# Nyström attention and a squared-ReLU feed-forward on one core: batch 0's A computed with whole-tile exponentials, another rule for warm-up products, and a new order table

## The chip, the cores and the metric

The kernel runs on 1 core of one Trainium2 chip. The metric is device time in microseconds (us) from launch to end, the median of several runs. A profiled execution has a time of its own and a span, which goes from its first to its last instruction. The five engines run instruction queues of their own: TensorE (PE; its weight loads are PEld), VectorE (DVE), ScalarE (ACT), GpSimd (POOL) and SyncE (SP). Each works its queue strictly in order and waits on semaphores for the others.

## The reference

For 8 batches of 8 heads (576 tokens, head size 64, 32 landmarks) the attention is approximated through landmark means, and its output goes through a two-layer feed-forward with the square of a ReLU between the layers.

```python
q_lm = q.reshape(B, H, m, S // m, D).mean(axis=3)      # m = 32, 18 tokens each
k_lm = k.reshape(B, H, m, S // m, D).mean(axis=3)
A = sm(q, k_lm); Bm = sm(q_lm, k_lm); C = sm(q_lm, k)  # sm: scaled softmax over the last axis
Z = Bm.T / (norm_1(Bm) * norm_inf(Bm) + 1e-06)
for _ in range(6):
    Z = 2 * Z - Z @ Bm @ Z
x = (A @ Z @ C @ v)                                    # then 4608 tokens x 512
h = x @ w_in                                           # 512 x 2048
out = (np.maximum(h, 0.0) ** 2) @ w_out                # 2048 x 512
```

## The kernel before, in words

The kernel is one core's program over the 8 batches. Nothing is scheduled by the compiler. Every piece of work is an "op" with a name, declared with `op(...)`, and the long string `ORDER` (line 1239) lists all names. `name@n` gives the PSUM banks, and `/A`, `/D`, `/P` put an op on ACT, DVE or POOL in place of its usual engine. `Plan.schedule` (line 100) walks the list once with rough durations and gives each op a planned start, and the program is emitted in that order with real semaphores between engines. So an engine's queue is the list, read for that engine alone.

The names that matter here, with the batch b as first number:

- Loads, all issued by POOL on one software queue: `ldq`, `ldk` (queries and keys, tile X, line 426), `ldv` (V, line 442), `win` (a quarter of w_in in two halves, line 450; `win10` and `win11` are quarter 1), `wout` (a quarter of w_out, line 457), `lx` (another view of q and k for the landmark sums of batches 3 to 7, XS, line 432).
- Attention: `T` (32x32 block transposes of q and k, DVE, line 471), `lm`/`lme`/`lmt` (landmark means on PE, eviction, transpose), `B…` (the softmax of Bm and its norms, many short DVE steps), `BBT`, `Yi`, `Zi` and then six rounds `N` on PE (line 718 for batches 0 and 1, 713 later) and `U` on DVE (line 727) for Z; in batches 2 to 7 each `N` also needs `bd` (line 650). `SC`/`SS` are the scores of C (and of A from batch 2 on), `Cmx`, `Cex`, `CT` their softmax, `CV` = C times V, `Zd`, `Zm`, `ZC` the product with Z, `W` = (Z C V) times w_in by quarters, evicted by `We` into the tile WP.
- A in batches 0 and 1, in two parts u = 0 (256 tokens of each half) and u = 1 (320): `bk` builds a block-diagonal operand (line 961), `SA` the scores on PE, then `Amx` (row maximum, line 974), `Asb` (subtract, line 985), `Aex` (exponential, ACT, line 987), `Asu`, `Arc` (sum and reciprocal), `Aml` (scale, line 994), `Ap` (transpose on PE, line 1005), `Ab` (eviction to the tile AT). Batch 0 cuts each of them in two, a and b.
- Feed-forward: `F` (AT times WP, line 1079; four products of 256 or 320 columns for batch 0, f + 16 being part u = 1), `R` (ReLU eviction, ACT or DVE), `Q` (square into the tile G), `O` (G times w_out, line 1126, four products of 512 columns each), `Oe` and `St` (eviction and store).

In batch 0 before, the part u = 1 takes another way through the exponential: `BY_ROW` (line 1229) names it, and `rows` (line 978) issues ten ACT exponentials of 32 columns for each half, each with its row's negated maximum (tile NM) as bias, so that no `Asb` is needed there. The row maxima of a and of b go to two tiles, NM1a and NM1b.

While TensorE has nothing to do early on, `Plan.fillers` (line 161) puts products of constants into the gaps of the planned PE times (line 1200, tile onesb), up to the first `O0` op. It takes an op's end as its start plus its duration.

Of the kernel before, what the change touches and what calls it, by code (L numbers as in the profile page):

```python
# [54 lines left out]
class Plan:  # L55
# [105 lines left out]
    def fillers(self, until, width, emit):  # L161
# [3 lines left out]
        for o in ops:  # L165
            a, b = o.start, o.start + o.engs["PE"]
# [43 lines left out]
def a_(n):  # L210
    return 0.1 + 0.00084 * n
# [53 lines left out]
def kernel(  # L265
# [32 lines left out]
    XS = mk("XS", [96, 2, H, 6, D], BF16)  # L298
# [22 lines left out]
    NM = {k: mk("NM" + "".join(map(str, k[1:])), [P, 10], F32) for k in BY_ROW}  # L321
# [139 lines left out]
    def attention(b):  # L461
# [17 lines left out]
        def landmarks_rows():  # L479
# [3 lines left out]
            def lmx(e):  # L483
                xs = XS[:].rearrange("p t (r c) j d -> p t r c j d", r=2)
# [7 lines left out]
               lambda e: copy(e, lm[:], view(), scale=LMS), R=[pl_], W=[("LM", i2, r) for r in range(2)])  # L492

# [445 lines left out]
        for u in range(2) if b in TOKENS else ():  # L939
# [27 lines left out]
            cuts = [0, 2 * n, 4 * n] if b in FIRST else [0, 4 * n]  # L967
            for j, (x0, x1) in enumerate(zip(cuts, cuts[1:])):
# [3 lines left out]
                by_row = (b, u, z) in BY_ROW  # L972
                op(f"Amx{b}.{u}{z}", {"DVE": v_(w)}, lambda e, s3=s3, p3_=p3_, pS=pS, at=at, neg=NM.get((b, u, z)):
                   nc.vector.tensor_reduce(s3(0)[:, at] if neg is None else neg[:, 0:at.stop - at.start],
                                           p3_(pS)[:, at], axis=AX.X, op=ALU.max, negate=neg is not None),
                   R=[pS], W=kx_("amx"))

                def rows(e, nm=NM.get((b, u, z)), sa3=sa3, p3_=p3_, pS=pS, x0=x0, x1=x1):
                    for x in range(x0, x1):
                        nc.scalar.activation(sa3[:, x], p3_(pS)[:, x], AF.Exp, bias=nm[:, x - x0:x - x0 + 1])  # L980
# [181 lines left out]
    def loads(what, b):  # L1162
# [53 lines left out]
ROWS = (3, 4, 5, 6, 7)  # L1216
SQ_POOL = (0,)
# [11 lines left out]
BY_ROW = ((0, 1, "a"), (0, 1, "b"))  # L1229
# [10 lines left out]
c0 ldk0.1 c1 ldq0.1 ldq0.0 ldk0.0 ldq1.0 ldk1.0 c2 ldk1.1 c12 c3/A c11 c5 T0.11 ldq1.1 ldv0.00  # L1240
ldv0.10 T0.01 c9/A lm0.1@1 c6/A c17 lmc0.10 lmc0.11/D ldv0.11 lme0.1 lmt0.1 T0.00 SC0.1@2 win00
T0.10 lm0.0@0 Cmx0.1 Bce0@6 win01 lme0.0 Cex0.1 lmt0.0 T1.00 bk0/P B0@4 SC0.0@0 c15/A Bmx0 Bsb0
CT0.1 Bex0 win11 Bsu0 SA0.1@2 Brc0 Cmx0.0 Bml0/P Bmb0/A c13 win10 Bcs0 Btr0 Cex0.0 Amx0.1a BBT0@5
Bnm0 SA0.0@7 Brn0 Aex0.1a c8 Yi0 Zi0/P Amx0.1b win21 Amx0.0b N0.0@0 lm1.0@4 U0.0 Amx0.0a Asb0.0b
N0.1@1 Aex0.1b lm1.0a U0.1 win20 Asb0.0a CT0.0 N0.2@6 lm1.0b U0.2 T1.01 win31 N0.3@5 lme1.0 win30
U0.3 CV0@6,0 Aex0.0a Asu0.1a lmt1.0 Asu0.0a bk1/P CVe0.0/A B1@2 Asu0.1b N0.4@4 c10 Aex0.0b U0.4
Bmx1 Arc0.1a Bsb1 N0.5@5 Asu0.0b Aml0.1a/P Bex1 SA1.1@6 c14/A Bsu1 Arc0.1b Brc1 CVe0.1/A Crc0
U0.5 wout0 Cmk0 Aml0.1b CR0@2 Amx1.1 Zd0@4 Bml1/P CRe0/A Bmb1/A Zm0 Ap0.1@2 Blo1 Arc0.0a Arc0.0b
Asb1.1 Aml0.0a/P Bcs1@0 Ab0.1/A SA1.0@5 Btr1 Aml0.0b/P Aex1.1 Bnm1 Bad1 BBT1@3 Brn1 ldv1.11 ZC0@4
Yi1 Ap0.0@7 Zi1 ZCe0 Amx1.0 wout1 N1.0@6 Ab0.0/A W0.1@2 U1.0 W0.0@0 ldk2.1 Asb1.0 We0.1 N1.1@4  # L1250
wout2 W0.2@6 U1.1 We0.01/D We0.00 ldk2.0 N1.2@5 F0.4@2 We0.2 U1.2 ldq2.0 F0.2@0 R0.4/D F0.0@4
# [120 lines left out]
```

## Time and profile before

| what | value |
|---|---|
| time, median of 3 runs | 259.07 us (259.05 to 259.97) |
| profiled execution, its own time | 259.55 us |
| its span | 257.8 us |
| PE, DVE, ACT, POOL busy | 248.5, 211.5, 176.3, 71.5 us |
| granted TensorE clock, mean | 0.999 |
| DMA moved | 34.18 MB, mean 133 GB/s |
| first F product starts | 30.49 us |
| first O product starts | 34.80 us |
| products of constants | 43 |

A row of the timeline reads: start in us, length in us, engine, line of the kernel, operation, tile written and tiles read, shape, count of merged instructions, and in brackets how long the engine stood idle before and what ended that. Rows of a stretch ("30.50:34.80 4.30, …") give its length and then the busy time and count of PE, PEld, DVE, ACT and POOL in that order, the granted clock, the share of the DMA engines and GB/s.

### The profile page before, as it was taken

To read this page: it belongs to the slowest core of one execution; us is meant where nothing else is said; L and a number is where in the kernel's file an instruction comes from. 1 tells how busy PE (TensorE), PEld (TensorE's weight loads), DVE (VectorE), ACT (ScalarE), POOL (GpSimd) and SP (SyncE) were. 2 spreads that over 40 slices of the span, in tenths; PEclk is the share of its full clock that TensorE was granted. 3 is DMA by queue.
4 is the path that set the end of the run, shared out by engine and by line. 5 is a ranking of instruction groups with operands and counts; after the bars stand their busy time and mean duration, and the time that the engine had idled before them with its cause. 6 is when DMAs were issued, how large, how long until landed. Compare 5 with 4: busy or idle time off the path is not lost.

```text
span 257.8 us, 7581 instructions
## 1 busy us (share of the span) xinstructions
PE 248.5 (96%) x3093; PEld 140.5 (54%) x3093; DVE 211.5 (82%) x549; ACT 176.3 (68%) x343; POOL 71.5 (28%) x122
## 2 busy tenths in 40 slices
PE   6979999999999999999999999999999999999993
PEld 2546565557554567465555466465454575466542
DVE  2779897987999999998998999888999989667221
ACT  3465779669896898888566499596663897357300
POOL 8566846643353260550210400021100100000000
PEclk9999999999999999999999999999999999999999
DMA  6999999999999999899613991025100350231044
GB/s 100 200 191 201 204 210 208 208 224 233 235 203 220 221 212 220 137 202 223 154 21 69 170 205 30 4 45 122 43 3 3 81 123 3 57 79 31 4 106 97
DMA packets 25123, 34.18 MB, mean 133 GB/s; under 512 B 2432, under 2 KB 14464, under 8 KB 25088
## 3 DMA queue, kind: packets, MB, share of 16 engines
q0 software_dynamic: 19168, 24.25, 55.6%
q1 hardware_dynamic: 5760, 9.31, 14.2%
q8 instruction: 24, 0.39, 0.6%
q10 hardware_dynamic: 160, 0.13, 0.2%
q14 instruction: 11, 0.09, 0.1%
HBM read 48.50 MB, written 9.44 MB: 225 GB/s over the span
## 4 chain that ended last, share of the span: by engine, by line
PE 84%; DVE 7%; DMA 3%; POOL 2%; issue 1%; ACT 1%; POOLq 0%
PE ps L1126 46%; PE ps L1079 23%; PE ps L906 3%; DMA X<-in_q_dram 3%; PE ps L835 2%; PE ps L487 1%; PE ps L749 1%; DVE SA L1032 1%; PE ps L713 1%; POOL X L426 1%; PE ps L1005 1%; PE ps L1200 1%; ACT SA L980 1%; PE ps L744 1%; PE ps L718 1%
## 5 line engine op out<-in xcount | busy, mean ns | idle before, releaser
L1126 PE MATMUL ps<-w_out,G 128*128 128x512 bf16 (+1 forms) x592 | 138.3, 374 | 0.0
L1126 PEld LDWEIGHTS <-G 128*128 128x128 bf16 x592 | 54.0, 98 | 54.7 <-issue 5.8
L1100 ACT ACTIVATE RS<-ps 128x576 bf16<-128x576 f32 (+2 forms) x104 | 63.7, 652 | 13.3 <-PE ps L1079 8.9
L1079 PE MATMUL ps<-AT,WP 128*128 128x288 bf16 (+2 forms) x512 | 72.0, 286 | 0.0
L1079 PEld LDWEIGHTS <-WP 128*128 128x128 bf16 x512 | 48.6, 98 | 20.6 <-issue 1.9
L1107 ACT ACTIVATE G<-RS 128x576 bf16<-128x576 bf16 (+2 forms) x54 | 35.9, 686 | 2.0 <-DVE RS L1102 1.6
L1109 DVE TENSOR_TENSOR G<-RS 128x576 bf16<-128x576 bf16 (+2 forms) x72 | 31.1, 447 | 6.8 <-ACT RS L1100 6.4
L471 DVE STREAM_TRANSPOSE TT<-X 128x576 uint32<-128x576 uint32 x32 | 24.0, 759 | 4.8 <-DMA X<-in_k_dram 4.2
L413 ACT CAST WP<-ps 128x1024 bf16<-128x1024 f32 (+1 forms) x23 | 21.8, 978 | 7.9 <-PE ps L906 7.8
L413 ACT COPY OS<-ps 128x512 f32<-128x512 f32 (+1 forms) x25 | 14.2, 571 | 18.1 <-PE ps L1126 18.0
L650 POOL TENSOR_TENSOR BD<-ST,blkb 128x256 bf16<-128x256 bf16 x15 | 10.9, 725 | 46.5 <-DVE ST L727 46.5
L790 ACT ACTIVATE C<-ps,sm 128x576 bf16<-128x576 f32 x16 | 14.4, 904 | 12.3 <-DVE sm L787 11.9
L1102 DVE TENSOR_SCALAR RS<-ps 128x576 bf16<-128x576 f32 (+2 forms) x24 | 17.9, 747 | 5.5 <-PE ps L1079 4.7
L442 POOL DMA_DIRECT2D V<-in_v_dram x24 | 12.9, 539 | 18.4 <-PE ps L835 15.1
L417 DVE COPY OS<-ps 128x512 f32<-128x512 f32 x12 | 8.3, 689 | 9.8 <-PE ps L1126 9.8
L727 DVE SCALAR_TENSOR_TENSOR ST<-ST,ps 128x128 bf16<-128x128 bf16 (+1 forms) x48 | 12.7, 264 | 2.6 <-PE ps L713 2.4
L1200 PE MATMUL ps<-onesb 128*128 128x512 bf16 (+1 forms) x38 | 11.9, 402 | 1.5 <-DVE onesb L349 1.5
L787 DVE TENSOR_REDUCE sm<-ps 128x1 f32<-128x576 f32 x16 | 11.8, 741 | 1.4 <-PE ps L718 1.2
L417 DVE CAST WP<-ps 128x1024 bf16<-128x1024 f32 (+1 forms) x11 | 12.2, 1119 | 0.3 <-PE ps L906 0.2
L1032 DVE STREAM_TRANSPOSE SA<-ps 128x320 f32<-128x320 f32 (+1 forms) x24 | 10.1, 456 | 0.3 <-PE ps L744 0.3
L906 PE MATMUL ps<-w_in,ZC 64*32 64x512 bf16 x256 | 10.2, 382 | 0.0
L426 POOL DMA_DIRECT2D X<-in_q_dram x16 | 8.9, 559 | 4.5 <-DVE sm L644 2.5
(144 smaller groups left out, 292.2 us busy)
## 6 DMA issues: line engine op xcount, KB each, us to landing
out_dram<-OS SPq DMA_DIRECT2D x70, 128.0 KB, 2.5
X<-in_k_dram POOLq DMA_DIRECT2D x16, 288.0 KB, 8.9
X<-in_q_dram POOLq DMA_DIRECT2D x16, 288.0 KB, 10.3
XS<-in_k_dram POOLq DMA_DIRECT2D x5, 576.0 KB, 9.6
XS<-in_q_dram POOLq DMA_DIRECT2D x5, 576.0 KB, 7.5
V<-in_v_dram POOLq DMA_DIRECT2D x8, 288.0 KB, 8.8
w_in<-in_moe_w_in_dram POOLq DMA_DIRECT2D x8, 256.0 KB, 10.3
w_out<-in_moe_w_out_dram POOLq DMA_DIRECT2D x4, 512.0 KB, 10.1
```

Source lines behind the costliest of these rows:

```text
L413: nc.scalar.copy(o, i)
L417: eng(e).tensor_copy(o, i)
L471: op(f"T{b}.{t}{r}", {"DVE": v_(576) + 0.02}, lambda e, r=r: nc.vector.transpose(tt[:, t, r].rearrange("p s m e -> p (s m e)").bitcast(U32 ...
L790: op(f"Cex{b}.{r}", {"ACT": a_(576) + 0.27}, lambda e, r=r: nc.scalar.activation(Cs[r][:].rearrange("p x u -> p u x"), cbanks(r), AF.Exp, ...
L906: nc.tensor.matmul(ps[quad(pos_a(c, r)), pW.at + r, :], lhsT=zcs[r][half, pos_c(c, r), :], rhs=w_in[half, c, 512 * ch:512 * ch + 512], sta ...
L1079: nc.tensor.matmul(ps[:, ph.at + i, 0:w], lhsT=wp[:, r, 128 * ff:128 * ff + 128], rhs=at[:, r, t0:t0 + w], start=(r == 0), stop=(r == 1))
L1100: nc.scalar.activation(rs, pair(ph, w), AF.Relu)
L1102: nc.vector.tensor_scalar(out=rs, in0=pair(ph, w), scalar1=0.0, scalar2=None, op0=ALU.max)
L1107: nc.scalar.activation(g, rs, AF.Square)
L1109: eng(e).tensor_tensor(g, rs, rs, ALU.mult)
L1126: nc.tensor.matmul(bank(po)[:, 0:c1 - c0], lhsT=G[:, f, lo:lo + P], rhs=w_out[:, f, c0:c1], start=(f == 0), stop=(f == NF - 1))
L1200: nc.tensor.matmul(ps[:, j, 0:w], lhsT=onesb[:, 0:P], rhs=x[:, 0:w], start=True, stop=True)
```

## The change

Four things are edited. The last covers the whole table.

First, `BY_ROW` is empty, so batch 0's part u = 1 goes through `Amx`, `Asb`, one `Aex` of 320 columns for each half, as u = 0 does: 20 ACT instructions become 2, and DVE gains the two subtractions `Asb0.1a` and `Asb0.1b`. Second, in `fillers` a PE op now ends where the plan says, with the wait for the next block of instructions that the plan counts for it, and not at start plus duration; 38 products of constants remain of 43. Third, the code for landmark sums added up by the DMA (`load_sums`, `landmarks_added`, `ADDED`) comes in, but `ADDED` is empty, so that it issues nothing; XS gets 128 partitions in place of 96, of which 96 are used. Fourth, `ORDER` is written anew for all batches.

```diff
-            a, b = o.start, o.start + o.engs["PE"]
+            a, b = o.start, o.end
...
-    XS = mk("XS", [96, 2, H, 6, D], BF16)
+    XS = mk("XS", [P, 2, H, 6, D], BF16)
...
-    NM = {k: mk("NM" + "".join(map(str, k[1:])), [P, 10], F32) for k in BY_ROW}
+    NM = mk("NM", [P, 20], F32)
...
+            by_row = (b, u) in BY_ROW
+            if by_row:
+                op(f"Amx{b}.{u}", {"DVE": v_(128 * n)}, lambda e, nm=NM, p3_=p3_, pS=pS, n=n: nc.vector.tensor_reduce(
+                    nm[:, 0:4 * n], p3_(pS), axis=AX.X, op=ALU.max, negate=True),
+                   R=[pS], W=[("NM", z) for z in range(2)])
...
                 if by_row:
-                    op(f"Aex{b}.{u}{z}", {"ACT": ROW * (x1 - x0)}, rows, R=[pS, *kx_("amx")], W=kx_("sa"))
+                    op(f"Aex{b}.{u}{z}", {"ACT": ROW * (x1 - x0)}, rows, R=[pS, ("NM", j)], W=kx_("sa"))
                 else:
+                    op(f"Amx{b}.{u}{z}", {"DVE": v_(w)}, lambda e, s3=s3, p3_=p3_, pS=pS, at=at:
+                       nc.vector.tensor_reduce(s3(0)[:, at], p3_(pS)[:, at], axis=AX.X, op=ALU.max),
+                       R=[pS], W=kx_("amx"))
                     op(f"Asb{b}.{u}{z}", {"DVE": v_(w)}, lambda e, sa3=sa3, p3_=p3_, pS=pS, b3=b3, at=at:
...
+ADDED = ()
+ADD_COST = 1.5
...
-BY_ROW = ((0, 1, "a"), (0, 1, "b"))
+BY_ROW = ()
...
-U0.5 wout0 Cmk0 Aml0.1b CR0@2 Amx1.1 Zd0@4 Bml1/P CRe0/A Bmb1/A Zm0 Ap0.1@2 Blo1 Arc0.0a Arc0.0b
+CVe0.0/A Aml0.0a/P T1.01 N0.4@5 CRe0/A CVe0.1/A wout0 U0.4 Asb0.1a bk1 B1@6 Aex0.1a ldq2.1
```

On PE the new table reads, from the end of batch 0's Z on: `N0.5 B1 Ap0.0 Zd0 SA1.0 ZC0 SA1.1 W0.1 W0.3 Ap0.1 F0.6 W0.0 F0.4 Bcs1 F0.20 F0.2 F0.0 F0.18 W0.2 F0.22 F0.16 F0.12 F0.14 O1.0 BBT1 F0.28 …`. The old one read `N0.5 SA1.1 CR0 Zd0 Ap0.1 Bcs1 SA1.0 BBT1 ZC0 Ap0.0 N1.0 W0.1 W0.0 N1.1 W0.2 N1.2 F0.4 F0.2 F0.0 W0.3 F0.18 F0.6 F0.22 F0.20 F0.10 O1.0 F0.24 …`. So part u = 0 of A comes first where u = 1 did, and batch 1's `BBT1`, `N1.0`, `N1.1` and `N1.2` have gone from ahead of the F products to behind the first O products. The pieces that follow show three other queues.

The first place is ACT's queue between the joint C V and the first ReLU evictions (L980 and L987 before, L1013 after are the exponentials, AT the eviction of A, ZC that of Z C V, WP that of W, RS the first ReLU). Before:

```order
L413 CAST Bb_107<-Bf_105 128x64
L413 CAST AT_80<-ps 128x640
L987 ACTIVATE SA_76<-SA_76 128x640
L413 CAST ZC_0_90<-ps 128x128
L413 CAST AT_80<-ps 128x512
L413 CAST WP_94<-ps 128x2x512
L413 CAST WP_94<-ps 128x512
```

And after:

```order
L1013 ACTIVATE SA_76<-SA_76 128x320 x2
L415 CAST AT_80<-ps 128x512
L607 ACTIVATE Bl_103<-Bl_103 128x64
L415 CAST ZC_0_90<-ps 128x128
L415 CAST Bb_107<-Bf_105 128x64
L1013 ACTIVATE SA_77<-SA_77 128x512
L415 CAST WP_94<-ps 128x2x512 x2
L1126 ACTIVATE RS_128<-ps 128x512
```

Between the eviction of Z C V and the first eviction of W now stand batch 1's `Bmb1` (Bb) and the exponential `Aex1.0` (SA_77, 512 columns); before, it was the eviction `Ab0.0` (AT, 512) alone. The two exponentials of batch 0's u = 1 (the first row, 320 columns) now stand behind C V, where before their twenty stood ahead of it. The eight copies of cpick, which stood second in ACT's queue before, now stand between the two exponentials of u = 0.

The second place is POOL's queue from the last quarter of w_in to the second half of w_out (An is `Aml`'s output, BK `bk`'s, w_out and X are loads). Before:

```order
L450 DMA w_in_123<-in_moe_w_in_dram 64x4x512 x4
L961 TENSOR_TENSOR BK_143<-LT1_75,blkw_142 128x512
L994 TENSOR_TENSOR An0_78<-SA0_76,smA0_119 128x320
L457 DMA w_out_124<-in_moe_w_out_dram 128x4x512
L590 TENSOR_TENSOR Bf1_105<-Bl1_103,sm1_118 128x64
L994 TENSOR_TENSOR An1_79<-SA1_77,smA1_120 128x256 x2
L442 DMA V1_66<-in_v_dram 32x1152
L457 DMA w_out_124<-in_moe_w_out_dram 128x4x512
```

And after:

```order
L462 DMA w_in_122<-in_moe_w_in_dram 64x4x512 x4
L1020 TENSOR_TENSOR An1_79<-SA1_77,smA1_120 128x256 x2
L469 DMA w_out_123<-in_moe_w_out_dram 128x4x512
L428 DMA X2_64<-in_q_dram 128x1152
L454 DMA V1_66<-in_v_dram 32x1152
L1020 TENSOR_TENSOR An0_78<-SA0_76,smA0_119 128x320
L469 DMA w_out_123<-in_moe_w_out_dram 128x4x512
L648 TENSOR_TENSOR Blo_108<-Bf1_105,Bb1_107 128x64
L1020 TENSOR_TENSOR An0_78<-SA0_76,smA0_119 128x320
```

The scalings of u = 0 (An1) moved ahead of those of u = 1 (An0), `bk1` (BK) went to DVE, and the last scaling, on which `Ap0.1` waits, now stands behind the issue of `wout1` (the second w_out row) and `Blo1`. Before it was on DVE.

The third place is DVE's queue while batch 2's Z is worked out and batch 1's F products begin (L727 and L750 are `U`; TT0 and TT1 are the transposes `T` of batches 2 and 3; BD is `bd`). Before:

```order
L671 TENSOR_TENSOR ST0_0_96<-Bf0_104,sm0_117 128x2x32
L471 STREAM_TRANSPOSE TT1_69<-X0_62 128x576
L727 SCALAR_TENSOR_TENSOR ST0_1_97<-ST0_0_96,ps_61 128x128
L417 CAST WP1_95<-ps_61 128x512
L417 CAST WP1_95<-ps_61 128x2x512
L471 STREAM_TRANSPOSE TT1_69<-X0_62 128x576
L727 SCALAR_TENSOR_TENSOR ST0_0_96<-ST0_1_97,ps_61 128x128
```

And after:

```order
L673 TENSOR_TENSOR BD0_100<-ST0_0_96,blkb_145 128x256
L483 STREAM_TRANSPOSE TT0_68<-X2_64 128x576
L1128 TENSOR_SCALAR RS1_126<-ps_61 128x512
L750 SCALAR_TENSOR_TENSOR ST0_1_97<-ST0_0_96,ps_61 128x128
L483 STREAM_TRANSPOSE TT1_69<-X0_62 128x576 x2
L750 SCALAR_TENSOR_TENSOR ST0_0_96<-ST0_1_97,ps_61 128x128
L673 TENSOR_TENSOR BD0_100<-ST0_0_96,blkb_145 128x256
```

One transpose of batch 2 came into this stretch, and a third one of batch 3 stands a little further on, 12 rows behind the last one printed and still ahead of the scores `SS2.0`, where before two of batch 3's four stood here and two behind the scores.

236 lines of the change are left out of this document (129 added, 107 removed).

## The prediction, made before the changed kernel ran

> **What bounds the kernel now.** First the page: the busy line (engine, us, share of the span, instructions) and the chain of work that ended last.
>
> ```profile
> PE 248.5 (96%) x3093; PEld 140.5 (54%) x3093; DVE 211.5 (82%) x549; ACT 176.3 (68%) x343; POOL 71.5 (28%) x122
> PE 84%; DVE 7%; DMA 3%; POOL 2%; issue 1%; ACT 1%; POOLq 0%
> ```
>
> TensorE is busy for 248.5 of 257.8 us and is 84% of the chain. A share is an average, so next I read the stretches of the span (start:end, length, then busy us and count of PE, PEld, DVE, ACT, POOL, granted clock, DMA share, GB/s).
>
> ```profile
> 15.00:20.00 5.00, 3.81 (x60) 2.44 (x59) 3.61 (x14) 4.42 (x22) 2.59 (x6) 1.00 1.08 180
> 30.50:34.80 4.30, 4.30 (x41) 3.07 (x41) 3.81 (x9) 4.14 (x7) 2.33 (x5) 1.00 1.21 205
> 34.80:64.30 29.50, 29.50 (x414) 17.72 (x411) 24.14 (x64) 21.80 (x43) 15.44 (x25) 1.00 1.17 217
> 64.30:80.30 16.00, 15.39 (x206) 8.00 (x206) 15.53 (x44) 14.84 (x28) 8.59 (x14) 1.00 1.18 217
> 120.80:253.90 133.10, 132.97 (x1483) 73.50 (x1481) 107.33 (x255) 84.25 (x151) 10.88 (x18) 1.00 0.35 70
> ```
>
> From the first F product on, PE is full in these rows but in 64.3 to 80.3, where 0.61 us is missing. So the time is the moment at which this stream starts, plus fixed PE work, plus what stalls it. The clock is 1.00 even at 15 to 20 us, where PE is emptiest. PE's timeline gives the start of the stream, the price of its pieces, and its two stalls (start, length, engine, line, operation; in brackets idle before and releaser).
>
> ```profile
> 28.17 0.66 PE L1005 MATMUL ps<-ident,An 128*128 128x128 bf16 x4
> 30.49 1.53 PE L1079 MATMUL ps<-AT,WP 128*128 128x256 bf16 x12
> 31.95 0.41 PE L906 MATMUL ps<-w_in,ZC 64*32 64x512 bf16 x8
> 34.80 1.03 PE L1126 MATMUL ps<-w_out,G 128*128 128x512 bf16 x4
> 35.66 1.69 PE L1079 MATMUL ps<-AT,WP 128*128 128x320 bf16 x12
> 40.33 1.03 PE L1126 MATMUL ps<-w_out,G 128*128 128x512 bf16 x4
> 41.29 0.70 PE L749 MATMUL ps<-TT,LT 32*32 32x288 bf16 x32
> 41.81 0.24 PE L718 MATMUL ps<-ST 32*32 32x64 bf16 x8
> 41.98 2.76 PE L1126 MATMUL ps<-w_out,G 128*128 128x512 bf16 x12
> 64.65 0.28 PE L749 MATMUL ps<-TT,LT 32*32 32x288 bf16 x1
> 65.50 0.27 PE L744 MATMUL ps<-TT,LT 32*32 32x256 bf16 x1 [0.56 <-ACT RS L1100]
> 79.56 0.30 PE L749 MATMUL ps<-TT,LT 32*32 32x288 bf16 x1
> 79.91 0.27 PE L744 MATMUL ps<-TT,LT 32*32 32x256 bf16 x1
> ```
>
> An O quarter takes 0.86 in the stream (34.80 to 35.66). An F of u = 1 takes 0.54: twelve products run 1.69 including the last one's drain of about 0.15. An F of u = 0 takes by the same reading (1.53 − 0.15) / 3 = 0.46; I use 0.44, since the drain of a last product is nearer 0.2. At 40.33 + 0.86 = 41.19 the quarter is through and the 32x32 scores start at 41.29: a change of tile shape costs 0.10. An N (L718) with its change back takes 0.17 (41.81 to 41.98). The two stalls are 65.50 − 64.65 and 79.91 − 79.56, less such a change and the first product's 0.1: about 0.64 and 0.14, together 0.78.
>
> **The head: what frees it.** The row exponentials hold ACT, and DVE waits for them.
>
> ```profile
> 5.33 2.01 ACT L413 COPY cpick<-identf 32x64 f32<-32x64 f32 x8
> 15.67 1.87 ACT L980 ACTIVATE SA<-ps,NM1a 128x32 f32<-128x32 f32 x10
> 18.10 1.89 ACT L980 ACTIVATE SA<-ps,NM1b 128x32 f32<-128x32 f32 x10 [0.56 <-DVE NM1b L974]
> 22.30 0.42 ACT L987 ACTIVATE SA<-SA 128x256 f32<-128x256 f32 x1
> 26.99 0.74 ACT L987 ACTIVATE SA<-SA 128x640 f32<-128x640 f32 x1 [0.25 <-DVE SA L985]
> 17.57 0.49 DVE L974 TENSOR_REDUCE NM1b<-ps 128x10 f32<-128x320 f32 x1 [1.33 <-ACT SA L980]
> 18.31 0.28 DVE L727 SCALAR_TENSOR_TENSOR ST<-ST,ps 128x128 bf16<-128x128 bf16 x1
> 24.02 0.20 DVE L727 SCALAR_TENSOR_TENSOR ST<-ST,ps 128x64 bf16<-128x64 bf16 x1
> 19.36 0.42 DVE L985 TENSOR_TENSOR SA<-ps,smA 128x256 f32<-128x256 f32 x1
> 26.13 0.77 DVE L985 TENSOR_TENSOR SA<-ps,smA 128x640 f32<-128x640 f32 x1
> ```
>
> Removed: 1.87 + 1.89 = 3.76 of ACT. Added: two exponentials of 320 columns, between 0.42 (256) and 0.74 (640), so 0.48 each, and on DVE two subtractions between 0.42 and 0.77, 0.49 each. But the 2.01 of cpick copies, which ran when ACT was free, now stands between u = 0's exponentials, so ACT's net relief here is 3.76 − 0.96 − 2.01 = 0.8. More matters on DVE: its idle 1.33 ahead of NM1b goes, and with it `U0.0` moves from 18.31 to about 16.9, and `U0.5`, the last step of Z, from 24.02 to about 22.5 (the chain N, U between them is unchanged, and DVE gains in it about what it loses). `bk1` is on DVE now, which no row shows; its bounds are 0.28 (`bd`, half as wide) and POOL's 1.17 for the same work. I take 0.42, nearer the DVE row.
>
> ```profile
> 25.49 0.41 DVE L861 TENSOR_TENSOR ZM<-ps,CRS 128x256 bf16<-128x256 f32 x1
> 29.26 0.68 DVE L985 TENSOR_TENSOR SA<-ps,smA 128x512 f32<-128x512 f32 x1
> 29.41 2.42 ACT L413 CAST WP<-ps 128x1024 bf16<-128x1024 f32 x3
> 23.31 0.73 POOL L994 TENSOR_TENSOR An<-SA,smA 128x320 bf16<-128x320 f32 x1
> 33.58 0.75 POOL L457 DMA_DIRECT2D w_out<-in_moe_w_out_dram  x1 [1.95 <-DMA w_out<-in_moe_w_out_dram]
> DMA to landing us min/median/max: 9.9/10.3/11.5
> L650 DVE TENSOR_TENSOR BD<-ST,blkb 128x256 bf16<-128x256 bf16 x21 | 5.9, 282 | 0.4
> 12.57 1.17 POOL L961 TENSOR_TENSOR BK<-LT,blkw 128x512 bf16<-128x512 bf16 x1
> ```
>
> Following that through: `Zm0` is at about 23.2 (was 25.49). `Asb1.0` moves up between `Zm0` and batch 1's norms and ends at 26.0 instead of 29.94. On ACT, `Aex1.0` and then `We0.1` follow at about 26.7 to 27.6 (was 29.41 to 30.4). Thus W is no longer what the first F waits for.
>
> **What is late next.** `F0.6` also needs `Ab0.1`, and so the transposes `Ap0.1`, and they need POOL's last scaling `Aml0.1b`, which stands behind three DMA issues: a load of X and one of V (shorter than a load of w_out, and taken while nothing waits) and `wout1`. The last one reuses the semaphore of the load eight before it, the last quarter of w_in, issued at about 15 in the new order; at 9.9 to 11.5 to landing (the row for those loads) it is free between 25.0 and 26.5. The row at 33.58, where a w_out issue held POOL for 1.95, shows that such a wait happens. Then `wout1` 0.75, `Blo1` (64 columns) 0.3 at most beside An's 0.73 for 320, and `Aml0.1b` 0.73: POOL is through between 26.8 and 28.3. With 0.66 for `Ap0.1` and what is left of the eviction, `F0.6` can start between 27.7 and 29.0. I take 28.6. Behind the waiting issue nothing else on POOL is urgent; DVE and ACT don't wait for it except through that eviction.
>
> From `F0.6` to `O1.0` the new order has six F of u = 0 (2.64), four of u = 1 (2.16), `W0.0` and `W0.2` (0.34 each, 31.95 to 32.29, with its change of shape) and `Bcs1` (0.28 at most, as it is no longer than those): 5.8. So `O1.0` starts at 34.4 to 34.5, with the bounds 33.75 (27.7 + 5.8, and 0.25 since W's evictions, 2.42 for three, then pace the first F) and 34.9; I take 34.45, against 34.80. What stands ahead of `O1.0` differs: F0.12, F0.14 and F0.16 came in and F0.10 went out (+0.98), `BBT1` and three N went behind it (−0.91: 0.17 for each, an estimated 0.06 more for the change ahead of it and what a thin piece loses at both ends). **Head: 34.80 − 34.45 + 0.07 = −0.42.**
>
> **Changes of tile shape.** In the stream behind `O1.0` I count 97 for 86, where batch pieces are now split by single O quarters; seven of the eleven are the moved `BBT1` and N, priced above, so four are new: 4 × 0.10 = **+0.38**. The Trainium skill, "TensorEngine Tiling (Array Packing)", section "Key Properties", says that changing the tiling mode, not just the tile, drains TensorE, and so speaks against finer interleaving. The row at 41.29 agrees, with 0.10; the sum would be the same by either.
>
> **The old stalls.** The 0.56 wait at 65.50 was for the ReLU that held the second bank of `SS2.1`. In the new order `O5.2`, `N2.5` and `O5.3` (0.86 + 0.1 + 0.86) stand between `SS2.0` and `SS2.1`, longer than the whole wait, and at 79.91 a similar step. **−0.78**, or nothing if the bank is late by as much again.
>
> **DVE ahead of `SS2.0`.** The batch-2 landmarks and transposes are the second place where it can go wrong.
>
> ```profile
> 54.70:64.30 9.60, 9.60 (x134) 5.97 (x130) 7.58 (x22) 8.65 (x17) 3.55 (x6) 1.00 1.15 236
> L471 DVE STREAM_TRANSPOSE TT<-X 128x576 uint32<-128x576 uint32 x32 | 24.0, 759 | 4.8 <-DMA X<-in_k_dram 4.2
> ```
>
> DVE is idle for 9.60 − 7.58 = 2.02 there, and the new order brings a net two transposes, 2 × 0.76 = 1.52, into it: 0.5 is left. They wait for X, too; its loads were issued earlier than before, which helps. I put +0.35 on all new stalls of the stream (none is shown by the trace; bounds 0 and the 1.52 of the transposes). The rest of the stream, the constants' 38 for 43 products and the wider XS, costs nothing on PE: the former lie in gaps of the head, and XS's new partitions hold nothing.
>
> **Sum.** −0.42 + 0.38 − 0.78 + 0.35 = −0.47 against the profiled run's own 259.55 (span 257.8 and 1.75 around it): 259.1. That run lies 0.48 over the median of 259.07, so on the median **258.6**.
>
> **Rivals.** *A, the head starts as early as W allows.* If quarter 3 of w_in lands after 9.9, `wout1` doesn't hold POOL, `F0.6` starts at 27.7, `O1.0` at 33.75: head −1.1. With no new stall the sum is −1.1 + 0.38 − 0.78 = −1.5: 257.6. For it: DVE and ACT both lose work ahead of the stream. Against it: the DMA share is 1.08 to 1.21 in the early stretches, so the queues are full, and the median landing is 10.3.
>
> *B, DVE becomes the bound at `SS2.0`; slower.* The place is the stretch ahead of 64.3. If DVE's idle 2.02 is made of waits for others (N's products, ReLU evictions) and can't be filled, the two transposes push the chain of batch 2's Z and the scores by up to 1.52, and as 64.3 to 80.3 is DVE-bound already (15.53 of 16.00), it isn't won back. It decides from 0.5 on, the slack that is left. PE then waits 1.5 and the old stall of 0.64 stays: −0.42 + 0.38 − 0.14 + 1.5 + 0.35 = +1.67: 260.7.
>
> *C, the clock.* Five products of constants fewer leave longer gaps in the head. If one of them let the clock fall for some 3 us, PE's work there would take about 1.5 longer: the head −0.42 would be +1.1, 260.1 to 260.5. Against: 1.00 at 15 to 20 with PE idle for 1.19. The Trainium skill, "TensorE: Matmul & The Clock Gate", section "Part 1: The HAM clock gate", has the clock halved after a stretch without matmuls; no row here shows that.
>
> *D, the change gives nothing.* The cpick copies take the place of the rows on ACT, or POOL's wait takes W's place entirely (`F0.6` at 29.0, `O1.0` at 34.9): head +0.1, 259.0 to 259.3.
>
> **How the numbers follow.** Forecast 0.47, D 0.08, both within 0.5% (1.3 us, about what a measurement can tell from no change): same 0.55. A 0.27: faster 0.27. B 0.14 and C 0.04: slower 0.18. The range goes from 257.3 (a little under A) to 260.8 (B): left out are a head better than its bounds and a B with further loss, about 0.15.
>
> **What would show it.** Right: no 1.33 wait on DVE at 17; `U0.0` near 16.9, `U0.5` near 22.5; a wait of POOL at `wout1` ahead of the last An; first F at 28.6 and first O at 34.45; no wait for RS in the second half of `SS2`; PE idle under 0.4 in 60 to 80; clock 1.00. Wrong: a first F later than 29.5, a wait of PE for TT ahead of `SS2.0` or `SS3.0`, an N of batch 2 waiting for ST by a microsecond, or a wait at an O for w_out, which I cost at nothing because no O waited for it before.

## The result and the profile after

| | before | changed |
|---|---|---|
| executions shown with the result | 20 | 20 |
| median, lowest, highest, us | 259.63, 259.02, 260.67 | 260.60, 258.88, 263.65 |
| profiled execution, its own time, us | 259.55 | 259.54 |
| granted TensorE clock in that one | 0.999 | 1.00 |

The changed kernel is slower: the ratio is 1.004, with the interval 1.0021 to 1.0058; it leaves out the two executions of 263.40 and 263.65, which count as slow. The forecast was 258.6, a small gain. But the two profiled executions took the same time, 0.01 us apart. What separates the medians is not in the profile after; it is in the list of executions, which gives each one's mean granted clock. The changed kernel was executed 30 times in all, here and in the two runs of it below; the kernel before has 93 in the four lists that stand beside the experiments.

| mean granted clock | changed: count, median, range | before: count, median, range |
|---|---|---|
| 0.996 to 1.00 | 5, 259.54, 258.88 to 260.62 | 92, 259.60, 259.04 to 261.18 |
| 0.990 to 0.993 | 15, 260.52, 260.01 to 262.57 | 1, 262.14 |
| 0.985 to 0.987 | 10, 262.00, 261.43 to 263.65 | 0 |

So at full clock the two kernels differ by no more than their spread, and 25 of 30 executions of the changed one lose clock. The profiled one is one of the five that don't. It still says how far the forecast's steps hold. First its stretches (columns as before):

```profile
30.50:34.80 4.30, 4.30 (x38) 2.66 (x35) 4.03 (x8) 3.91 (x7) 2.79 (x4) 1.00 1.19 207
34.80:64.30 29.50, 29.50 (x426) 17.21 (x424) 25.87 (x71) 21.40 (x40) 12.60 (x23) 1.00 1.18 220
64.30:80.30 16.00, 16.00 (x214) 7.99 (x212) 15.59 (x45) 12.60 (x23) 10.35 (x17) 1.00 1.17 215
80.30:120.80 40.50, 39.96 (x543) 23.00 (x555) 37.59 (x105) 34.82 (x64) 13.94 (x24) 1.00 0.98 188
120.80:253.50 132.70, 132.56 (x1480) 72.91 (x1471) 106.05 (x248) 86.70 (x153) 15.08 (x23) 1.00 0.38 74
```

The hole of 0.61 at 64.3 to 80.3 is gone, as forecast, and new ones of 0.54 and 0.14 stand behind 80.3, where before had none. (The last row ends at 253.50, as the changed kernel's last product ends at 253.56 and that of before at 253.77; the 0.13 that before lacks in its row up to 253.90 is this end.) Then TensorE's timeline in the head:

```profile
16.92 0.24 PE L741 MATMUL ps<-ST 32*32 32x64 bf16 x8 [1.30 <-POOL ST L694]
25.63 0.20 PE L902 MATMUL ps<-ZM,CV 128*64 128x32 bf16 x1 [1.18 <-issue]
28.12 0.61 PE L1105 MATMUL ps<-AT,WP 128*128 128x256 bf16 x4
34.03 1.03 PE L1152 MATMUL ps<-w_out,G 128*128 128x512 bf16 x4
```

The first F starts at 28.12 (before 30.49) and `O1.0` at 34.03 (before 34.80). In front of them stand two idle stretches that before did not have in this form: 1.30 ahead of `N0.0`, for a POOL operation, and 1.18 in the middle of `ZC0`, where the releaser is "issue": the profile shows nothing that TensorE waits for. Before has one shorter wait of this second kind:

```profile
26.62 0.20 PE L630 MATMUL ps<-Bb,blkb 128*128 128x64 bf16 x1 [0.39 <-issue]
```

In the changed kernel, the rows of POOL, DVE and ACT behind the forecast's steps are these, engine by engine:

```profile
15.94 0.61 POOL L462 DMA_DIRECT2D w_in<-in_moe_w_in_dram  x1 [1.17 <-DMA X<-in_k_dram]
16.56 0.30 POOL L694 TENSOR_TENSOR ST<-Bf,sm 128x64 bf16<-128x64 f32 x1
25.77 0.82 POOL L469 DMA_DIRECT2D w_out<-in_moe_w_out_dram  x1 [0.37 <-DMA w_in<-in_moe_w_in_dram]
26.89 0.73 POOL L1020 TENSOR_TENSOR An<-SA,smA 128x320 bf16<-128x320 f32 x1
17.26 0.29 DVE L750 SCALAR_TENSOR_TENSOR ST<-ST,ps 128x128 bf16<-128x128 bf16 x1 [0.87 <-PE ps L741]
22.56 0.40 DVE L984 TENSOR_TENSOR BK<-LT,blkw 128x512 bf16<-128x512 bf16 x1
23.02 0.20 DVE L750 SCALAR_TENSOR_TENSOR ST<-ST,ps 128x64 bf16<-128x64 bf16 x1
25.87 0.27 ACT L415 CAST ZC<-ps 128x128 bf16<-128x128 f32 x1 [1.72 <-PE ps L902]
27.05 1.93 ACT L415 CAST WP<-ps 128x1024 bf16<-128x1024 f32 x2
```

`Zi0` (the 0.30 on POOL) stands behind the issue of `win31`, which waited 1.17 for a load to land; that is what held `N0.0`. And ACT stood 1.72 idle until `ZC0` was through.

### The profile page after: what moved, and what is told of

Its sections match the earlier page's. It is cut to its first block, busy times and chain, and to the rows that moved or that the text cites. A ratio compares the mean times of both kernels' runs of the same rounds, so it can differ in the third digit from the quotient of the medians.

```text
span 257.6 us, 7553 instructions
## 1 busy us (share of the span) xinstructions
PE 247.8 (96%) x3088; PEld 139.3 (54%) x3088; DVE 212.3 (82%) x543; ACT 174.7 (68%) x325; POOL 75.9 (29%) x130
## 4 chain that ended last, share of the span: by engine, by line
PE 75%; DVE 13%; DMA 6%; POOL 2%; issue 2%; ACT 1%; DVEq 0%; POOLq 0%; ACTq 0%
PE ps L1152 42%; PE ps L1105 20%; DMA w_in<-in_moe_w_in_dram 4%; PE ps L929 3%; DVE G L1135 2%; PE ps L858 2%; DMA X<-in_q_dram 2%; PE ps L772 1%; DVE SA L1058 1%; DVE sm L810 1%; PE ps L736 1%; PE ps L499 1%; DVE RS L1128 1%; DVE smA L1069 1%; DVE ZM L892 1%
## 5 line engine op out<-in xcount | busy, mean ns | idle before, releaser
L1126 ACT ACTIVATE RS<-ps 128x576 bf16<-128x576 f32 (+2 forms) x101 | 61.7, 651 | 12.0 <-PE ps L1105 6.5
L1133 ACT ACTIVATE G<-RS 128x576 bf16<-128x576 bf16 (+2 forms) x57 | 37.7, 686 | 1.5 <-DVE RS L1128 1.1
L1135 DVE TENSOR_TENSOR G<-RS 128x576 bf16<-128x576 bf16 (+2 forms) x69 | 30.1, 452 | 3.5 <-ACT RS L1126 2.8
L415 ACT COPY OS<-ps 128x512 f32<-128x512 f32 (+1 forms) x30 | 17.2, 580 | 23.2 <-PE ps L1152 22.8
L673 POOL TENSOR_TENSOR BD<-ST,blkb 128x256 bf16<-128x256 bf16 x18 | 13.5, 747 | 37.9 <-DVE ST L750 32.5
L415 ACT CAST WP<-ps 128x1024 bf16<-128x1024 f32 (+1 forms) x24 | 22.6, 982 | 2.5 <-PE ps L929 2.4
L1128 DVE TENSOR_SCALAR RS<-ps 128x576 bf16<-128x576 f32 (+2 forms) x27 | 20.1, 758 | 4.7 <-PE ps L1105 3.3
L750 DVE SCALAR_TENSOR_TENSOR ST<-ST,ps 128x128 bf16<-128x128 bf16 (+1 forms) x48 | 12.7, 265 | 7.4 <-PE ps L736 3.8
L1230 PE MATMUL ps<-onesb 128*128 128x512 bf16 (+1 forms) x33 | 10.3, 403 | 1.6 <-DVE onesb L351 1.6
L419 DVE CAST WP<-ps 128x1024 bf16<-128x1024 f32 (+1 forms) x10 | 11.0, 1109 | 0.2
L428 POOL DMA_DIRECT2D X<-in_k_dram x16 | 9.1, 574 | 4.2 <-DMA w_out<-in_moe_w_out_dram 1.8
```

What stands on the lines that cost most here:

```text
L415: nc.scalar.copy(o, i)
L428: lambda e: nc.gpsimd.dma_start(x[:, t, r].rearrange("p s d -> p (s d)"), src),
L1126: nc.scalar.activation(rs, pair(ph, w), AF.Relu)
L1128: nc.vector.tensor_scalar(out=rs, in0=pair(ph, w), scalar1=0.0, scalar2=None, op0=ALU.max)
L1133: nc.scalar.activation(g, rs, AF.Square)
L1135: eng(e).tensor_tensor(g, rs, rs, ALU.mult)
```

## The experiments

**The changed kernel again, and products in its two idle stretches.** The theory was that the clock gate halves TensorE's clock behind an idle stretch; the rival, that the new order's stream simply stalls more. The code added ahead of an op is in each case of this form:

```diff
     pl.fillers(FILL_UNTIL(pl), 0.11, fill)
+    for name, n in (("N0.0", 10), ("ZC0", 8)):
+        i = next(i for i, o in enumerate(pl.order) if o.name == name)
...
+        f.emit = lambda e, j=j, n=n: fill(j, n, False)
+        pl.order.insert(i, f)
```

j is a PSUM bank that is free there. e2 has N0.0 alone, e3 ZC0 alone, e4 both.

The changed kernel again. 

> The changed kernel as it is, run again. Theory G (the clock gate): its undisturbed executions (mean granted clock 1.00) took 258.9 to 259.5, as fast as before, and the others showed a mean clock of 0.985 to 0.997 and 260.1 to 262.6; so again most executions show a mean clock below 1, each 0.007 of it (one stretch of about 3.4 us at half clock, 0.007 x 258 = 1.8) goes with 1.5 to 1.9 us, the median is 260.2 to 261.2, and if the profiled execution is one of these, its low clock stands within 15 to 30 us. Rival S (the new order's stream stalls more): the executions spread over 258.9 to 262 at one clock, and the profile shows PE waits behind 34 us of 1 us or more.

Measured: 261.43 median (259.60 to 262.04), a little above the forecast, ratio 1.0057 (1.0034 to 1.0081). Its profiled execution was one at clock 0.993, of 260.91. Its stretches of one us each, PE being the first count and the granted clock the figure before the last two:

```profile
23.00:24.00 1.00, 1.00 (x16) 0.85 (x13) 1.00 (x6) 1.00 (x4) 0.55 (x1) 1.00 1.28 217
24.00:25.00 1.00, 0.42 (x9) 0.28 (x7) 0.94 (x6) 0.19 (x2) 0.23 (x1) 1.00 1.20 195
25.00:26.00 1.00, 0.00 (x0) 0.00 (x0) 1.00 (x3) 0.00 (x0) 0.98 (x2) 1.00 1.25 204
26.00:27.00 1.00, 0.81 (x9) 0.65 (x9) 0.85 (x3) 0.56 (x3) 0.91 (x3) 0.82 1.23 208
27.00:28.00 1.00, 1.00 (x22) 0.34 (x20) 0.46 (x1) 0.40 (x1) 1.00 (x3) 0.50 1.26 205
...
29.00:30.00 1.00, 1.00 (x7) 0.43 (x4) 1.00 (x2) 1.00 (x2) 0.36 (x2) 0.50 1.28 220
30.00:31.00 1.00, 1.00 (x17) 0.59 (x16) 0.43 (x2) 0.81 (x3) 0.43 (x1) 0.97 1.21 201
```

In the wait for instructions (here 1.70, from 24.50 to 26.20) PE is empty, and then the clock is 0.50. From (1 − 0.82) / 0.5 + 3 + (1 − 0.97) / 0.5 the half clock lasts 3.42 us. Laid beside the undisturbed execution product by product, this one is 0.56 late at `ZC0`'s last product, 1.08 at the first F product, up to 1.48 just behind it, and 1.33 to 1.37 from 33 us to the end: the block came 0.56 later and the half clock took another 0.8. The rival falls; nothing is lost behind 36 us. But the loss for one stretch at half clock, 1.37, is below the 1.5 to 1.9 expected.

Products at `N0.0`. 

> Changed kernel, with products of constants worth 10 units (1.1 us) in TensorE's idle stretch of 1.30 us at 15.6, ahead of N0.0, which waits for POOL there. Theory G with this gap as the cause: mean clock 1.00 in nearly all executions, median 258.9 to 259.4. Theory G with the other gap (24.5 to 25.6, an instruction block) as the cause: no better than the changed kernel, 260.2 to 261.2. Rival S: 260.2 to 261.2, clock as the changed kernel's.

Products at `ZC0`. 

> Changed kernel, with products of constants worth 8 more units (0.9 us) ahead of ZC0, in whose middle TensorE waits 1.18 us for a block of instructions at 24.5. Theory G with this gap as the cause: mean clock 1.00 in nearly all executions, median 258.9 to 259.6 (the products may cost up to 0.2 themselves). With the first gap as the cause: 260.2 to 261.4. Rival S: 260.2 to 261.4.

Both. 

> Changed kernel with both sets of products. Theory G, whichever gap or both: mean clock 1.00 in nearly all executions and a median of 258.9 to 259.6, spread under 1 us. Rival S: 260.2 to 261.4, spread as the changed kernel's.

| run | median (range) | executions at clock 0.996 or more |
|---|---|---|
| e2, at N0.0 | 260.72 (259.90 to 262.84) | 6 of 12 |
| e3, at ZC0 | 260.19 (259.17 to 260.63) | 12 of 12 |
| e4, both | 260.91 (260.71 to 260.97) | 6 of 6 |

The ratios to before are 1.0037 (1.0011 to 1.0064), 1.0008 (0.9993 to 1.0023) and 1.0046 (1.0030 to 1.0062). Covering the wait at `ZC0` cures the clock, covering the one at `N0.0` halves the cases at most. But e3's and e4's times did not come down to the expected 258.9 to 259.6. TensorE's rows of e3 show why:

```profile
25.65 0.27 PE L902 MATMUL ps<-ZM,CV 128*64 128x32 bf16 x5 [0.72 <-issue]
51.30 0.20 PE L879 MATMUL ps<-ST,dupm 128*128 128x64 bf16 x1
51.94 0.20 PE L879 MATMUL ps<-ST,dupm 128*128 128x64 bf16 x1 [0.43 <-issue]
```

The four products brought a second wait of the same kind, at 51.94, and e2 and e4 have one there too (0.56 and 0.59; e2's row names an operation of ACT as its releaser, but it ends at the same place in the count). This changed the theory: the waits sit at fixed places in the count of TensorE's instructions. In the program's order the one in the head stands at about its 690th in before and in every variant (in the traces' rows of products and weight loads, of which some can be missing, the 694th to 702nd), whatever operation that is (`Bcs1` before, `ZC0`'s eighth product in the changed kernel, its third in e3). The page's DMA queues show what is waited for:

```profile
q8 instruction: 24, 0.39, 0.6%
```

24 transfers of 16 KB in all; TensorE's rows are 3088 products and as many weight loads, 6176, so there is one transfer for some 256 of them. The traces date these transfers. The one for the place in the head ran from 24.20 to 25.16 us in before and from 23.32 to 24.30 in the changed kernel. In all sixteen profiled executions the first product behind that place starts 1.3 to 1.5 us after its transfer has ended, however long TensorE has been idle, and the one behind the second wait 1.4 to 1.5 after its own (e2 to e5). So what is waited for is this block of instructions. Between TensorE's passing of one boundary (about its 434th instruction) and the first instruction behind the next there lie 5.62 in before (21.00 to 26.62), 5.32 in the changed kernel (20.31 to 25.63), 5.84 in its second run, and 5.1 to 6.1 in all others. TensorE itself needs only 3.96 for these 256 in the changed kernel (20.31 to 24.27), where before it took 4.85, with products of constants standing at the end. The new order made Z's chain faster up to a boundary whose block had not come.

**The rule for products of constants, both ways round.**

```diff
-            a, b = o.start, o.end
+            a, b = o.start, o.start + o.engs["PE"]
```

e5 is this edit of the changed kernel; e10 is its reverse in the kernel before.

The old rule in the changed kernel. 

> Changed kernel with the old counting rule for products of constants: six more products (1.2 us) behind the stalled ZC0, ahead of W0.1; nothing else moves. Theory G (TensorE waits for an instruction block at its instruction 690 or so, and the clock gate halves the clock behind that idle stretch): the products stand behind the stall, so it stays, the clock is below 0.996 in a third of the executions or more, W0.1 is up to 1.2 later, and 12 instructions more put the block boundary near 51 us ahead of an O, as in the runs with added products, for 0.4 to 0.7 more: median 260.8 to 262.3. Rival N (it is the number of the products, 38 for 43): clock 1.00 throughout, median 258.9 to 259.6.

The new rule alone in the kernel before. 

> The kernel before with the new counting rule alone: three products fewer (ahead of BBT1, at 27.2 us), all else in its place, six instructions fewer from there on. Rival N (the number of products is what costs): clock below 0.996 in a third of the executions or more, median 260.2 to 261.2. Theory G: the idle stretch that arises is 0.6 us behind a wait of 0.4 and at most a few executions fall below 0.996; median 259.3 to 260.2.

Measured: e5 263.09 (260.70 to 263.66), 4 of 6 executions at 0.991 to 0.993; e10 259.60 (258.61 to 260.21), 12 of 12 at 0.997 or more, ratio 0.9997 (0.9984 to 1.0011). The number of products is not the cause. The old rule would have put 1.2 us of them behind the wait, where they hold up W, and e5 is the slowest of all, above its forecast (ratio 1.0109, 1.0070 to 1.0148); one of its two executions at full clock took 262.81, so its loss is not the clock's alone. The new rule is worth having with this order. In e5's profiled execution the clock fell behind the other idle stretch, the one at 16:

```profile
16.00:17.00 1.00, 0.05 (x2) 0.09 (x1) 0.83 (x3) 0.98 (x4) 0.60 (x1) 1.00 1.08 203
17.00:18.00 1.00, 0.62 (x13) 0.52 (x12) 0.28 (x2) 0.95 (x5) 0.96 (x3) 0.99 1.15 202
18.00:21.00 3.00, 3.00 (x29) 1.58 (x27) 1.80 (x9) 0.69 (x3) 2.19 (x5) 0.50 1.19 186
```

**The first edit alone, and the idle stretch put into the kernel before.**

```diff
-BY_ROW = ((0, 1, "a"), (0, 1, "b"))
+BY_ROW = ()
-... Aex0.1a ... Aex0.1b ...
+... Asb0.1a Aex0.1a ... Asb0.1b Aex0.1b ...
```

e6 is the kernel before with this and all its products kept in their places.

> The kernel before with the first edit alone: whole-tile exponentials for batch 0's u = 1, its two subtractions put right ahead of them in the old table; TensorE's order and all 43 products are those of before. Theory G: DVE's wait of 1.33 goes and TensorE comes to its instruction 690 some 0.5 to 1.5 sooner, but the block comes 5.3 to 5.9 after the boundary before it, so its wait there grows from 0.4 to between 0.8 and 1.5 and little is gained: median 259.2 to 260.2 with before at 259.6, and more executions below clock 0.996 than before has (1 of 26). Rival R (the removal by itself is worth the 0.4 that was forecast for the head, and only the new order loses it): median 258.7 to 259.2, clock 1.00.

Measured: 259.50 (258.52 to 260.94), ratio 0.9994 (0.9973 to 1.0016), clock 0.997 or more in 12 of 12. Its TensorE rows:

```profile
25.66 0.20 PE L630 MATMUL ps<-Bb,blkb 128*128 128x64 bf16 x1
31.43 0.41 PE L906 MATMUL ps<-w_in,ZC 64*32 64x512 bf16 x8 [0.37 <-DMA w_in<-in_moe_w_in_dram]
34.28 1.03 PE L1126 MATMUL ps<-w_out,G 128*128 128x512 bf16 x3
```

The head gains 0.52 (`O1.0` at 34.28 for 34.80), of which 0.28 is lost again at 101 us, in the landmark sums of a later batch; the median moves by 0.15 us. The wait at the block did not grow to the 0.8 expected. It shrank to 0.11 (25.55 to 25.66), where before has 0.39: TensorE comes to it 0.68 sooner, but the block's transfer, too, ran 0.84 sooner (from 23.36, for 24.20). So the first edit's gain shows in the head of one trace, and in the median it is not clear of noise; it costs no clock.

e8 keeps TensorE's count and order in the kernel before and moves five products from around its own wait for the block to the idle stretch ahead of `N0.1`. In units of 256 columns, 2 ahead of `Ap0.1`, 2 ahead of `Bcs1` and 5 ahead of `BBT1` go, and 10 come in ahead of `N0.1`.

> The kernel before with five products (9 units) taken from between 25 and 28 us, around its wait for the instruction block, and five of 512 put ahead of N0.1 at 17.6, where it idles: count of instructions and order of all else are those of before. Theory G: an idle stretch like the changed kernel's arises at 25.5 to 27, and the clock is below 0.996 in a third of the executions or more, 0.8 to 1.8 each: median 259.8 to 261. Rival S (the new order's stream is what costs): 259.3 to 259.9, clock 1.00.

Measured: 261.35 (259.33 to 262.89), a little above the forecast, ratio 1.0050 (1.0017 to 1.0082), 7 of 8 executions at 0.984 to 0.990. Its profiled one, of 262.89:

```profile
25.00:27.00 2.00, 1.37 (x17) 0.97 (x17) 2.00 (x7) 0.45 (x3) 0.88 (x3) 1.00 1.24 195
27.00:28.00 1.00, 0.74 (x21) 0.62 (x20) 0.82 (x5) 1.00 (x2) 1.00 (x3) 0.69 1.23 204
28.00:34.00 6.00, 6.00 (x81) 3.02 (x79) 3.65 (x10) 4.12 (x7) 4.58 (x8) 0.50 1.23 207
34.00:35.00 1.00, 1.00 (x13) 0.51 (x6) 1.00 (x3) 0.51 (x1) 0.56 (x2) 0.90 1.16 211
```

The old order loses its clock as well once its cover is gone, for 0.62 + 6 + 0.2 = 6.82 us, twice 3.41. Laid beside before, this execution has lost 2.05 us by 36 us, and it is 3.38 late at the end. The other 1.33 come at one place far behind, where TensorE waits for the loads of a later batch's landmark sums:

```profile
104.80 0.84 PE L487 MATMUL ps<-XS,seg 96*32 96x256 bf16 x24 [1.29 <-DMA XS<-in_k_dram]
```

Whether the half clock delayed that load is not shown. Neither the new order nor its stream is needed for the clock to fall.

**Cover without a change of count, and the POOL operation moved.** e7 takes four products from the warm-up (7.6 and 11.0 us) to `ZC0`; e9 takes seven, three of them to `N0.0`; e13 moves `Zi0` on POOL ahead of the load that held it, as below; e14 is e13 with e7's products.

```diff
-... win31 BBT0@7 ... Asb0.0b Zi0/P Yi0 ...
+... BBT0@7 ... Asb0.0b Zi0/P win31 Yi0 ...
```

> Changed kernel with four products of 512 moved from the warm-up at 7.6 and 11.0 us to the place ahead of ZC0: the clock cover of the run with 8 units more, but TensorE's instruction count is as in the changed kernel. Theory G with the block boundaries: clock 0.996 or more in nearly all executions, no wait at L879 near 51 us, median 258.9 to 259.6. Rival P (the added products cost what that run lost, 0.6 or so, by themselves): 259.9 to 260.4.

> Changed kernel with seven products of 512 moved inside the head, TensorE's instruction count kept: four to ZC0 and three to N0.0 (the idle 1.30 us at 15.6), taken from the covered stretches at 5.6, 7.6, 11.0 and 12.5 us. Theory G (both idle stretches let the clock fall, the one at 15.6 too): clock 0.996 or more in all but one or two executions (four products at ZC0 alone: 9 of 12), median 258.9 to 259.5, highest below 261. If the idle stretch at 15.6 doesn't matter: about 3 of 12 executions stay at 0.99 to 0.993 and 261.5 to 262.3.

> Changed kernel with one POOL operation moved: Zi0 (0.30 us) ahead of the load win31, whose issue waits 1.17 us for a landing at 14.8 to 15.9 and holds Zi0, and with it N0.0, to 16.9. TensorE's order and products are those of the changed kernel. Theory G: the idle 1.30 us at 15.6 goes, Z and the boundary at instruction 434 come 0.8 to 1.2 sooner and the block at 690 with it, so the first F starts 0.3 to 1.0 sooner; the idle stretch at 690 stays at 1.0 to 1.7, so the clock is still below 0.996 in a third to two thirds of the executions, but seldom below 0.990; best executions 258.2 to 258.8, median 259.2 to 260.6. Rival Q (the wait at 15.6 is covered by later ones, above all W's loads and POOL): first F at 28.0 to 28.3 and best executions as the changed kernel's, 258.9.

> The same with four products of 512 moved from 7.6 and 11.0 us to ZC0, count kept. Theory G: with the stretch at 15.6 gone and that at 690 partly covered, clock 0.996 or more in at least 10 of 12 executions; median 258.3 to 259.2, faster than before (259.4 to 259.75) and than the changed kernel. Rival Q: 259.0 to 259.5. If other stretches of the head let the clock fall: 3 or more of 12 below 0.996.

| run | median (range) | at clock 0.996 or more | ratio to before (interval) |
|---|---|---|---|
| e7, four products to ZC0 | 259.40 (258.83 to 262.23) | 9 of 12 | 1.0006 (0.9976 to 1.0035) |
| e9, and three to N0.0 | 259.93 (259.31 to 262.01) | 8 of 12 | 1.0024 (1.0000 to 1.0047) |
| e13, Zi0 first | 261.48 (259.01 to 262.51) | 1 of 9 | 1.0053 (1.0022 to 1.0085) |
| e14, Zi0 first and four products | 259.44 (259.14 to 262.45) | 11 of 12 | 1.0007 (0.9987 to 1.0027) |

e7's wait at 51 is gone, as the count demands, and its nine full-clock executions have a median of 259.20. e9 was a miss: the products at `N0.0` did not help, and its profiled execution still waited 1.2 at the block, which came at 26.15. e13 was a miss, too: without the wait for `Zi0`, `N0.0` starts 0.95 sooner (15.97 for 16.92), but the next step then waits for a load, the wait at the block stays, and the clock falls in 8 of 9. Its TensorE rows:

```profile
16.90 0.81 PE L523 MATMUL ps<-X,ident 128*128 128x256 bf16 x6 [0.47 <-DMA X<-in_q_dram]
25.12 0.23 PE L902 MATMUL ps<-ZM,CV 128*64 128x32 bf16 x1 [0.98 <-issue]
```

So most of the changed kernel's losses hang on the stretch at the block, and with both stretches treated (e14) 11 of 12 executions keep their clock, between 259.14 and 259.83. That is the time of before (259.46 beside it), as rival Q had it, and not less. With twelve executions each, 9, 8 and 11 don't tell e7, e9 and e14 apart. No version here beats the kernel before beyond the interval.

**Two more profiled executions**, for where executions differ. 

> The kernel before, one look, for where its executions at full clock differ by up to 1.5 us (259.1 to 260.6). Theory G: in the head, by when an instruction block or a load comes in, by 0.3 to 1.2 at the wait at instruction 690 or at the first loads, the stream behind it being the same within 0.3. Rival S: by waits spread over the stream.

> The changed kernel, one look more. Theory G: if its mean clock is below 0.996, half clock stands for 3.4 us, or twice that, within 6 us behind the idle stretch at 15.6 or at 24.5, and 1.2 to 3.5 us are lost there against the undisturbed execution; if it is 1.00, the time is 258.8 to 260. Rival S: at a low clock too, most of the loss lies behind 36 us.

e11 took 259.30 at clock 0.997; TensorE passed the boundary 0.18 sooner than in the first execution of before (26.43 for 26.62) and the end is 0.23 sooner. That fits the theory, but one execution does not settle what spreads before over 259.0 to 260.6 at full clock; it stays open. e12 took 261.55 at 0.993: 1.03 was lost up to the first O, where the theory has it, and another 0.95 at 49 to 51 us, where it has nothing. The rows there, first DVE's and POOL's of e12, then DVE's of the undisturbed execution:

```profile
48.29 1.27 DVE L837 TENSOR_TENSOR CMX<-cmk,sm 128x16 f32<-128x16 f32 x1
50.24 0.42 DVE L553 SCALAR_TENSOR_TENSOR LM<-ps,LS 128x256 bf16<-128x256 f32 x1
48.46 1.06 POOL L1020 TENSOR_TENSOR An<-SA,smA 128x512 bf16<-128x512 f32 x1
```

```profile
47.26 0.17 DVE L837 TENSOR_TENSOR CMX<-cmk,sm 128x16 f32<-128x16 f32 x1
```

An operation of 0.17 took 1.27 and ended where POOL's scaling ended (48.29 + 1.27 = 49.56, and 48.46 + 1.06 = 49.52). In the undisturbed execution that scaling starts at 48.61, well behind the DVE operation; in e12 the stream comes 1.03 later, POOL does not, and the two meet. The profiled executions of e13 and e14 show the same, 0.99 and 1.52 for that operation, so part of the gap between a light and a heavy loss is this. A late stream does not always meet it: in e1 POOL's scaling was later too (49.27), and the operation took 0.17. It was seen in three traces and not tested by an edit. The Trainium skill, "SBUF — State Buffer", section "SBUF: two separate sides", says that VectorE with two SBUF inputs and GpSimd take a shared port pair as an exclusive lock for a whole instruction, whichever starts first. The common ends agree with the lock; who came first is not clear from the rows, as DVE's operation starts 0.17 ahead of POOL's in e12.

## Why the prediction was wrong, by its own steps

- **The head, −0.42: right in kind, too small in the undisturbed execution.** By the same working it measured −(34.80 − 34.03 + 0.07) = −0.84. `U0.5` came at 23.02 for 22.5, because `Zi0` was held behind `win31` on POOL: I had followed POOL's queue at `wout1` and not there. `bk1` took 0.40 on DVE for the 0.42 taken. POOL's chain ended at 27.62, inside 26.8 to 28.3, but the step that F0.6 needs it through `Ab0.1` was wrong: F0.6 belongs to u = 0. It only stands behind `Ap0.1` in TensorE's queue, and it started at 28.12, not 28.6, right behind `Ap0.1` and the first of W's two evictions (27.05, two in 1.93).
- **The old stalls, −0.78: right in kind.** PE is full at 64.3 to 80.3; all that it lacked there was 0.61.
- **New stalls, +0.35: mis-sized.** Behind 80.3 PE idles 0.54 + 0.14 = 0.68, where before it idled nothing. Rival B's place, ahead of `SS2.0`, shows none of it. With the changes of tile shape at +0.38, which no run measured by itself, the terms make −0.84 − 0.61 + 0.68 + 0.38 = −0.39. TensorE's last product ends only 0.21 sooner (253.56 for 253.77), so 0.18 more of busy time stands behind `O1.0` than the sum has; no run says in which pieces. e7's and e14's full-clock executions (medians 259.20 and 259.38) lie 0.1 to 0.5 under the medians of before beside them.
- **The base was off.** The last 0.48, from 259.1 down to 258.6, was taken off because the profiled execution of before lay that far over a median of three, 259.07. Over twenty the median is 259.63, and that execution is a usual one.
- **The step that failed is the clock, rival C, at 0.04.** It was put aside with "1.00 at 15 to 20 with PE idle for 1.19", a single execution, and sought in the five products of constants fewer. The runs show that the number of products is innocent (e10, e5) and that the cause is a wait that the sum has no term for: TensorE's wait for its next block of instructions, 1.18 in the undisturbed execution. In 25 of 30 executions the changed kernel loses clock, and in both of them that were profiled (e1, e12) the half clock follows this wait. The row with "[0.39 <-issue]" stood in the profile of before at that very boundary. The plan in both kernels has the blocks, too (`BLOCK` = 256 in `Plan`, with 6.2 us from one to the next in the first 140 us), and the second edit is about them. Z's chain was forecast to come 1.5 sooner at its end, and nothing in the working asked whether TensorE's instructions would.
- The price given to C, about 1.5 and 260.1 to 260.5, was near: 1.0 for one drop (260.52 against 259.54) and 2.5 for two or for one and a collision. The rule of "TensorE: Matmul & The Clock Gate" of the Trainium skill, section "Part 1: The HAM clock gate", quoted there as not shown, is borne out by e1, e5 and e8 in kind: half clock, for 3.42 us or twice that, where the Trainium skill gives about 3.4 for its window. But it has the clock fall after an idle window, and here TensorE idled only 1.77 us in the 3.41 ahead of the fall in e1, and 1.34 in e5.

## What to carry to other kernels

Ahead of a stream that keeps TensorE full, ask of every gain not only which wait comes next but whether the instructions are there: count TensorE's instructions, look for "issue" waits, and see which operation falls on that count after the change. Such a wait can cost twice, by itself and by the clock behind it (0.56 and 0.8 in e1), if nothing covers it. And one profiled execution at full clock is no proof that a kernel keeps it: read the list of clocks of all executions.

## What the runs showed of the hardware

- TensorE's next 256 instructions came 5.1 to 6.1 us after it had passed the boundary before, while loads kept the DMA queues full (share 1.2), and 1.3 to 1.5 us after the block's transfer had ended; products of constants count among the 256, so that four or more of them brought a wait of 0.4 to 0.6 at a place 25 us later (e2 to e4 against e7).
- The half clock came in pieces of about 3.41 us, one or two. They began at the end of an idle stretch (e13, 25.02 for 25.12; e1, 26.64 for 26.20) or up to 3 us behind it (e14, 28.42 for 25.55).
- The traces' clock records show a grid in this. Counted from the first record of its trace, the half clock begins at a whole multiple of 3.413 us in all eight profiled executions that have it (e1: 6.16 + 6 × 3.413 = 26.64; e5: 4.33 + 4 × 3.413 = 17.98; e14: 4.52 + 7 × 3.413 = 28.41), at the end of the interval that holds the idle stretch. That first record lies anywhere from 4.33 to 7.64, so the same stretch falls into these intervals otherwise in each execution. This would explain why only some executions of one kernel lose their clock; no edit tested it.
- Idle time alone does not say how empty such an interval must be: the kernel before idles 1.05 in one piece at 17.6, and held 0.996 or more in 92 of 93 executions, and e4 kept its clock with a wait of 1.30 beside its products. An estimate from the traces does better: each product counted with 0.215 us for 512 columns (a quarter of the 0.86 of four) and with the part of the 128 × 128 array that it uses. The interval ahead of the fall then holds 0.30 to 0.36 of a full array's work in all eight; the emptiest without a fall hold 0.35, 0.35, 0.36 and 0.37, that of the undisturbed changed kernel 0.38, and that of before 0.44. Why e8 and e13 stay at half clock for a second interval, in which TensorE is busy, is open.
- A DVE operation of 0.17 took 0.99, 1.27 and 1.52 beside a POOL operation of 1.06.
